# Attention, experts and a gated layer in one launch: the branch for extra tokens moves behind the first expert, and factors and weights are made during the experts

## The chip, the core and the metric

One core of one Trainium2 chip runs the whole program in one launch. The metric is the device time of an execution in microseconds (us). Engines: TensorE (PE, with PEld for its weight loads), VectorE (DVE), ScalarE (ACT), GpSimd (POOL) and SyncE (SP), which here issues nearly all DMAs.

## What is computed

```python
# 1: attention with random features: 4 batches, 8 heads, 576 tokens, 64 wide
h = x @ omega.T - sum(x * x) / 2;  phi = exp(h - max(h)) / sqrt(128)
x = (q_p @ (k_p.T @ v)) / (q_p @ sum(k_p) + 1e-6)       # 2304 tokens x 512
# 2: 8 experts, each token goes to one
e = argmax(normed(x) @ normed(emb).T / tau);  gate = softmax at e
x = gate * (relu(x @ w1[e]) @ w2[e])                     # w1 512 x 1024
# 3: gated layer; its weights are float64
g = x @ w_gate                                           # 512 x 1536
out = (g / (1 + exp(-g)) * (x @ w_val)) @ w_out          # 1536 x 512
```

All matrix products of the three layers that matter here are made from high and low parts: each factor is split into a hi part of a shorter mantissa and a lo part, and three matmuls (hi hi, hi lo, lo hi) stand for one.

## The kernel before

**Layer 1** runs in an order written out by hand and is not touched. Everything behind it is ordered, engine by engine, by the framework's scheduler, which simulates the program with a model of costs and can move an instruction far ahead of its place in the code; within an engine the order is then fixed. Buffers are tiles of pools: a load into a tile waits for the last reader of the tile before it.

**Layer 2.** The tokens are 4 blocks `bt` of S = 576 (one batch each). A block has a dominant expert, and all its tokens go through that expert with a gate of 0 where they belong to another (`expert`, L871). An expert is 8 units: 4 of `mm1` (L828) and 4 of `mm2` (L851), each with 48 matmuls of 288 columns and with one pair of loaded weights (`fetch`, `pair_tile`; hi by ACT at L90, lo by DVE at L91). ACT makes relu's hi and DVE its lo (L844, L845). Behind each mm2 DVE multiplies by the gate: into y_f at once (L869), or, where y_f is added to (`add`), into t, which POOL adds (L866, L867).

Tokens of a block that belong to other experts are the extra tokens: they are computed in a branch, `tc.If(totals[0] > 0)` (L940), with loops over blocks and experts inside. With the data of the runs shown the branch isn't taken. All engines meet at it. It stands ahead of the last block's expert, whose y_f is zeroed before it.

**Layer 3** uses a scheme of seven products for a 2 x 2 split of features and tokens. `split_y(bt)` (L883) makes seven factors of a block of x from y_f by four differences, each factor as hi (ACT) and lo; the lo and the differences of blocks 0 and 1 are POOL's, those of 2 and 3 DVE's but for two. `convert` (L729) turns a 128 x 512 piece of doubles, loaded as pairs of 32-bit words into a buffer of the experts' weights (tag raw), into float32 by eight DVE operations. `seven` (L776) makes the seven factors of the first weights of one f (12 chunks f of 128 hidden features): sums on POOL, hi on ACT, lo on POOL. Then `tokens` (L994): for each f, blocks in two pairs, seven products of six matmuls of 288 columns (L1041); DVE adds results from PSUM (L1006, L1012), ACT copies and takes silu, POOL makes one addition of two (L1013), and the hidden values go to DRAM (`hds`). The output phase reads them back (`hidden`, L1069), splits them (hi ACT, lo POOL) and multiplies them by the third weights (L1080), 8 + 8 + 2 tiles of 128 tokens, 512 columns; the third weights are converted during the first 8.

Of the kernel before, what the change touches and what calls it, by code (L numbers as in the profile page):

```python
# [27 lines left out]
def attention_moe_ffn_kernel(  # L28
# [688 lines left out]
    h_all = hpool.tile([128, F // 128 * 2 * S], F32R, name="h_all")  # L717
    LAST = B - 1

    def factor(bt, q, a):  # L720
        at = ((bt * 7 + q) * 2 + a) * S
        for v in (arena, h_all, late.get("x")):
            if at < v.shape[1]:
                return v[:, at:at + S].rearrange("p (c n) -> p c n", c=2)
            at -= v.shape[1]

    wf = {}

    def convert(dst, f, m):  # L729
# [2 lines left out]
        nc.sync.dma_start(
            out=raw, in_=w64[f, m].bitcast(I32).rearrange("p (n w) -> p n w", w=2)
        )
        t, a = (late["cpool"].tile([128, DM], I32, tag=k, name="cv_" + k) for k in "ta")
        low, high = raw[:, :, 0], raw[:, :, 1]
        nc.vector.tensor_scalar(  # L737
            out=t, in0=high, scalar1=0x7FFFFFFF, scalar2=None, op0=ALU.bitwise_and
        )
        nc.vector.scalar_tensor_tensor(  # L740
            out=high.bitcast(F32), in0=t.bitcast(F32), scalar=F64_LEAST,
            in1=high.bitcast(F32), op0=ALU.is_ge, op1=ALU.mult,
        )
# [434 lines left out]
```

## Time and profile before

| what | value |
| --- | --- |
| median of 3 runs | 842.24 us (840.14 to 843.22) |
| the profiled execution | 841.22 us |
| its span | 839.5 us |
| PE busy | 784.8 us, 93% |
| DVE busy | 555.1 us, 66% |
| POOL busy | 348.7 us, 42% |
| ACT busy | 340.0 us, 41% |
| mean granted clock of PE | 0.974 |

The span runs from the first to the last instruction of the execution on the core; the rest of its time lies around it. Busy shares are means over stages with different limits, so the stages have to be read apart. A granted clock of 1.00 is TensorE's upper level (2.4 GHz), 0.50 the lower one (1.2 GHz). In rows of a timeline the bracket gives the idle time before the instruction and what ended it; DVEq, ACTq and PEq stand for the sequencers of the engines, at a branch above all. Matmuls overlap, so the duration of a group is not its pitch.

### The profile page before, as it was taken

The page shows a single profiled execution, that of the slowest core. Times are in us where ns is not written, and L with a number is a line of the kernel's source. Part 1 is how long each engine was busy: PE and PEld are TensorE (multiplying, and loading weights), DVE is VectorE, ACT ScalarE, POOL GpSimd, SP SyncE. Part 2 cuts the span into 40 slices and gives each one's busy share as a digit, 9 for nine tenths or more (in the row PEclk, how much of TensorE's full clock was granted, in tenths as well). Part 3 has the DMA queues.
Part 4 walks back from the last instruction along what each step waited for, and adds up shares of the span by engine and source line. Part 5 has one row for each costly group of instructions (what it writes and reads, how often), then busy time and mean ns, then how long its engine had stood idle before and what let it go on. Part 6 is the DMA issues. An engine that isn't in the chain of part 4 may idle for free.

```text
span 839.5 us, 16157 instructions
## 1 busy us (share of the span) xinstructions
PE 784.8 (93%) x6364; PEld 729.2 (87%) x6365; DVE 555.1 (66%) x947; ACT 340.0 (41%) x823; POOL 348.7 (42%) x347
## 2 busy tenths in 40 slices
PE   9999899899999987986988889999999999789998
PEld 8878777899999987986988889999999987568886
DVE  6788998563424328868999977877893589960000
ACT  5887687331313222524333334444434522232123
POOL 4855253200000018765755635555555534234441
PEclk9999999999999998997999999999999999999999
DMA  8645540423223212510423333232231435335224
GB/s 282 201 143 176 186 157 22 115 78 90 86 92 90 79 32 75 135 52 0 128 83 102 109 111 95 103 107 93 109 116 73 143 122 159 140 113 183 86 68 150
DMA packets 35644, 94.13 MB, mean 112 GB/s; under 512 B 4432, under 2 KB 8544, under 8 KB 35560
## 3 DMA queue, kind: packets, MB, share of 16 engines
q1 hardware_dynamic: 35400, 92.99, 34.6%
q8 instruction: 52, 0.85, 0.4%
q14 instruction: 32, 0.26, 0.1%
q10 hardware_dynamic: 160, 0.02, 0.0%
HBM read 74.05 MB, written 18.95 MB: 111 GB/s over the span
## 4 chain that ended last, share of the span: by engine, by line
PE 32%; DVE 19%; issue 5%; POOL 3%; DMA 2%; ACT 1%; DVEq 0%; ACTq 0%; POOLq 0%; SPq 0%
PE a L1041 11%; PE o_ps L1080 10%; PE b L1041 5%; PE c L1041 3%; DVE cv_t L744 2%; DVE cv_a L748 2%; DVE cv_t L754 2%; DVE raw L740 2%; DVE cv_t L758 2%; PE two L857 2%; DVE cv_t L737 1%; POOL wl L91 1%; DVE raw L751 1%; DVE h_all L91 1%; DMA hds<-cc 1%
## 5 line engine op out<-in xcount | busy, mean ns | idle before, releaser
L1080 PE MATMUL o_ps<-xp 128*128 128x512 f32 x648 | 152.1, 397 | 8.2 <-ACT xp L90 7.9
L1080 PEld LDWEIGHTS o_ps<-xp 128*128 128x128 f32 x648 | 123.5, 191 | 36.6 <-ACT xp L90 10.0
L1041 PE MATMUL a<-xp,wh 128*128 128x288 f32 x432 | 92.4, 306 | 18.3 <-DVE c L1006 6.5
L91 POOL TENSOR_TENSOR xp<-h,xp 128x1024 fp32r<-128x1024 f32 (+1 forms) x36 | 67.1, 1866 | 101.4 <-ACT xp L90 101.4
L838 PE MATMUL two<-xp,wp 128*128 128x288 f32 x576 | 85.6, 309 | 9.5 <-ACT wp L90 4.7
L838 PEld LDWEIGHTS two<-xp,wp 128*128 128x128 f32 x576 | 82.8, 200 | 10.3 <-ACT wp L90 4.9
L91 POOL TENSOR_TENSOR xp<-y_f,xp 128x576 fp32r<-128x576 f32 x14 | 23.6, 1708 | 162.8 <-ACT xp L90 162.8
L491 ACT ACTIVATE ph<-two,bias 128x128 f32<-128x128 f32 x288 | 78.1, 387 | 29.5 <-DVE bias L482 23.2
L1041 PEld LDWEIGHTS a<-xp,wh 128*128 128x128 f32 x432 | 70.9, 194 | 21.5 <-DVE c L1006 8.0
L1009 ACT ACTIVATE cc<-cc 128x288 f32<-128x288 f32 x96 | 42.4, 445 | 106.6 <-DVE cc L1006 88.5
L1013 POOL TENSOR_TENSOR cc<-c,cc 128x288 f32<-128x288 f32 x48 | 45.7, 963 | 93.6 <-ACT cc L1009 91.0
L91 POOL TENSOR_TENSOR wl<-w,wh 128x512 fp32r<-128x512 f32 (+1 forms) x48 | 63.3, 1329 | 34.0 <-ACT wh L90 29.2
L90 ACT CAST wp<-raw 128x1024 fp32r<-128x1024 f32 x32 | 33.6, 1050 | 81.3 <-PE two L857 37.5
L1041 PE MATMUL a<-xp,wl 128*128 128x288 f32 x216 | 64.7, 303 | 0.2 <-POOL wl L91 0.2
L90 ACT CAST xp<-h 128x1024 fp32r<-128x1024 f32 (+1 forms) x36 | 30.1, 837 | 64.5 <-PE o_ps L1080 48.2
L857 PE MATMUL third<-h_all,wp 128*128 128x288 f32 x384 | 52.5, 296 | 0.0
L857 PE MATMUL two<-h_all,wp 128*128 128x288 f32 x384 | 51.8, 296 | 0.0
L857 PEld LDWEIGHTS third<-h_all,wp 128*128 128x128 f32 x384 | 51.6, 189 | 0.0
L857 PEld LDWEIGHTS two<-h_all,wp 128*128 128x128 f32 x384 | 51.4, 189 | 0.0
L474 DVE TENSOR_REDUCE mx<-two 128x8 f32<-128x1024 f32 x36 | 43.9, 1220 | 8.2 <-PE two L464 8.0
L91 DVE TENSOR_TENSOR wp<-raw,wp 128x1024 fp32r<-128x1024 f32 x30 | 40.3, 1344 | 12.5 <-ACT wp L90 11.8
L786 POOL TENSOR_TENSOR w<-w 128x256 f32<-128x256 f32 x48 | 44.6, 929 | 2.5
(199 smaller groups left out, 1738.9 us busy)
## 6 DMA issues: line engine op xcount, KB each, us to landing
raw<-in_w_dram SPq DMA_DIRECT2D x68, 512.0 KB, 3.6
hds<-cc SPq DMA_DIRECT2D x48, 288.0 KB, 2.1
h<-hds SPq DMA_DIRECT2D x24, 512.0 KB, 3.5
q<-in_qx_dram SPq DMA_DIRECT2D x18, 512.0 KB, 3.8
k<-in_kx_dram SPq DMA_DIRECT2D x14, 512.0 KB, 4.3
v<-in_vx_dram SPq DMA_DIRECT2D x18, 276.0 KB, 4.4
out_dram<-o SPq DMA_DIRECT2D x18, 256.0 KB, 3.4
h<-hds SPq DMA_DIRECT2D x12, 128.0 KB, 2.1
```

Of the source, the lines that this page charges most:

```text
L90: nc.scalar.copy(hi, src)
L91: lo_eng.tensor_tensor(out=lo, in0=src, in1=hi.bitcast(F32), op=ALU.subtract)
L474: nc.vector.tensor_reduce(out=mx.rearrange("p (c a) -> p a c", a=2), in_=p.rearrange("p a (h m) -> p a h m", m=M), axis=AX.X, op=ALU.max,)
L491: nc.scalar.activation(out=ph[:, h, :], in_=p[:, h % 2, h // 2 * M:(h // 2 + 1) * M], func=AF.Exp, bias=bias[:, h:h + 1],)
L740: nc.vector.scalar_tensor_tensor(out=high.bitcast(F32), in0=t.bitcast(F32), scalar=F64_LEAST, in1=high.bitcast(F32), op0=ALU.is_ge, op1=AL ...
L786: nc.gpsimd.tensor_tensor(out=out, in0=x, in1=y, op=op)
L838: nc.tensor.matmul(ps[:, j], w[:, a, c, f * 128:(f + 1) * 128], xv[:, c, b, j * HB:(j + 1) * HB], start=(c == 0 and n == 0), stop=(c == NC ...
L857: nc.tensor.matmul(ps[:, j], w[:, a, f, :], h[:, b, j * HB:(j + 1) * HB], start=(f == 0 and n == 0), stop=(f == len(hs) - 1 and n == 2),)
L1009: nc.scalar.activation(out=x, in_=x, func=AF.Silu)
L1013: nc.gpsimd.tensor_tensor(out=cc[:, 1], in0=c22, in1=cc[:, 1], op=ALU.mult)
L1041: nc.tensor.matmul(bank_of[k], wf[f][a][:, (wq * 2 + c) * 128:(wq * 2 + c + 1) * 128], factor(bt, xq, x)[:, c], start=(k not in begun), st ...
L1080: nc.tensor.matmul(p, h[:, x, i * 128:(i + 1) * 128], wos[f][:, a], start=(f == 0 and k == 0), stop=(f == NF - 1 and k == 2),)
```

## The change

Five things. The branch moves from ahead of the last expert to behind the matmuls of the first one (a hook ahead of its last gating), and y_f of blocks 1 to 3 is zeroed early, so that experts 1 to 3 all take the way with t and POOL's addition. The factors of x of block 0, 1, 2 are made during expert 1, 2, 3, in place of inputs that are no longer needed (`over_x`, `over_h`, `over_y`); those of block 3 behind expert 3; all lo and differences are DVE's. `convert` takes two doubles at once: one ACT operation (absolute value) and six DVE operations of 1024 columns; it has a buffer of its own. The first weights' lo moves from POOL to DVE. The first weights of f = 0 and 1 are converted during the experts, f + 2 during f, and the third weights in pairs ahead of their use.

```diff
-        n_pair[0] += 1
-        own = n_pair[0] % 3 == 0 or n_pair[0] == B * (NU + NC)
-        pool = late["cpool"] if own else wpool
+        n = n_pair[0] = n_pair[0] + 1
+        pool = late["cpool"] if n == 3 or (n > 3 and n % 3 == 2) else wpool
...
-    def convert(dst, f, m):
-        raw = wpool.tile([128, DM, 2], I32, tag="raw", name="raw64")
...
+    def convert(key, *doubles):
+        raw = late["w"].tile([128, 2, DM, 2], I32, tag="raw64", name="raw64")
+        for j, (f, m) in enumerate(doubles):
+            nc.sync.dma_start(
+                out=raw[:, j], in_=w64[f, m].bitcast(I32).rearrange("p (n w) -> p n w", w=2)
+            )
+        low, high = raw[:, :, :, 0].bitcast(U32), raw[:, :, :, 1]
+        t = late["t"].tile([128, 2, DM], I32, tag="raw", name="cv_t")
+        w = w32[key] = late["w"].tile([128, 2, DM], F32, tag="w32", name="w32", bufs=2)
+        nc.scalar.activation(out=t.bitcast(F32), in_=high.bitcast(F32), func=AF.Abs)
         nc.vector.tensor_scalar(
-            out=t, in0=high, scalar1=0x7FFFFFFF, scalar2=None, op0=ALU.bitwise_and
+            out=t.bitcast(F32), in0=t.bitcast(F32), scalar1=F64_ZERO, scalar2=None, op0=ALU.max
+        )
+        nc.vector.tensor_scalar(
+            out=t, in0=t, scalar1=0x07FFFFFF, scalar2=3,
+            op0=ALU.bitwise_and, op1=ALU.logical_shift_left,
         )
         nc.vector.scalar_tensor_tensor(
...
+            out=w.bitcast(I32), in0=high, scalar=-0x40000000, in1=t,
+            op0=ALU.bitwise_and, op1=ALU.bitwise_or,
         )
         nc.vector.tensor_scalar(
...
+            out=high, in0=w.bitcast(I32), scalar1=-0x800000, scalar2=None, op0=ALU.bitwise_and
         )
         nc.vector.scalar_tensor_tensor(
...
+            out=t.bitcast(F32), in0=low, scalar=2.0 ** -52, in1=high.bitcast(F32),
+            op0=ALU.mult, op1=ALU.mult,
+        )
+        nc.vector.tensor_tensor(out=w, in0=w, in1=t.bitcast(F32), op=ALU.add)
...
+    def weights_ahead(f):
+        if f < NF:
+            convert(f, (f, 0), (f, 1))
...
-            hi_lo(*(p[:, q * half:q * half + n] for p in parts), src, nc.gpsimd)
+            hi_lo(*(p[:, q * half:q * half + n] for p in parts), src)
...
             for d in range(NC):
-                mm2(x, hs, d, add)
+                ps = mm2(x, hs)
                 hooks.get(NU + d, lambda: None)()
+                gated(x, ps, d, add or (x.bt == 0 and d == NC - 1))
...
-            eng = nc.vector if bt >= LAST - 1 else nc.gpsimd
...
+        def extras():
+            xs[1].fetch()
+            routed.close()
...
+            with tc.If(totals[0] > 0):
...
+            nc.gpsimd.memset(y_f[0][:, NC - 1], 0.0)
+            for bt in range(1, B):
+                nc.gpsimd.memset(y_f[bt], 0.0)
...
+        todo = {
+            (0, 0): routing_end, (0, NU + NC - 1): extras,
+            (1, NU - 1): split0,
+            (2, 0): lambda: weights_ahead(0), (2, NU - 1): split1,
+            (3, 0): lambda: weights_ahead(1), (3, NU - 1): split2, (3, NU + 2): lambda: seven(0),
+        }
...
+        next(ends[2], None)
+        split(3, [over_h(r) for r in range(2, 16)])
+        next(ends[3], None)
...
                 if bt == 0 and f + 1 < NF:
-                    wf[f + 1] = seven(weights_of(f + 1, sp), parts_of(f + 1))
+                    seven(f + 1)
+                elif bt == 0:
+                    out_weights(0)
+                else:
+                    weights_ahead(f + 2)
+                    if f + 2 >= NF:
+                        out_ahead(2 * (f + 2 - NF))
...
                         if f not in wos:
-                            out_weights(f, op)
+                            out_weights(f)
+                        if f % 2 == 0:
+                            out_ahead(f + 4)
```

Which instructions stand where is settled by the scheduler. VectorE's order just ahead of the branch, before (the last lines of expert 2; L91 the lo of weights, L869 gating, L922 and L940 the branch):

```order
L869 TENSOR_TENSOR y_f<-two,gate 128x576
L91 TENSOR_TENSOR wp<-raw,wp 128x1024
L869 TENSOR_TENSOR y_f<-two,gate 128x576
L91 TENSOR_TENSOR wp<-raw,wp 128x1024
L869 TENSOR_TENSOR y_f<-third,gate 128x576
L922 TENSOR_LOAD tot_i
L940 COMPARE_AND_BRANCH
```

And after (the last lines of expert 0; L93 the lo of weights, L876 gating, L753 to L771 the six operations of a conversion, w_6254 its result, L939 and L926 the branch):

```order
L876 TENSOR_TENSOR y_f<-two,gate 128x576
L93 TENSOR_TENSOR wp<-raw,wp 128x1024
L753 TENSOR_SCALAR cv_t<-cv_t 128x1024
L756 TENSOR_SCALAR cv_t<-cv_t 128x1024
L760 SCALAR_TENSOR_TENSOR w_6254<-raw_6250,cv_t 128x1024
L876 TENSOR_TENSOR y_f<-two,gate 128x576
L93 TENSOR_TENSOR wp<-raw,wp 128x1024
L764 TENSOR_SCALAR raw_6250<-w_6254 128x1024
L767 SCALAR_TENSOR_TENSOR cv_t<-raw_6250 128x1024
L771 TENSOR_TENSOR w_6254<-w_6254,cv_t 128x1024
L939 TENSOR_LOAD tot_i
L926 COMPARE_AND_BRANCH
```

The last gating of the expert has left the place ahead of the branch, and a conversion stands there; that of f = 1, w_6254, is its last operation.

SyncE's queue ahead of the branch, before (L374 the experts' weights, L922 and L940 the branch):

```order
L374 DMA raw<-in_w_dram 128x1024
L363 TENSOR_LOAD dom_i
L374 ISA
L374 DMA raw<-in_w_dram 128x1024
L374 ISA
L374 DMA raw<-in_w_dram 128x1024
L922 TENSOR_LOAD tot_i
L940 COMPARE_AND_BRANCH
```

And after (L375 the experts' weights, raw_5749, raw_6250 and raw_6990 the doubles of f = 0, 1 and 2, L939 and L926 the branch):

```order
L327 DMA gts<-gt_t 72x128
L746 DMA raw_5749<-in_w_dram 128x1024 x2
L364 TENSOR_LOAD dom_i
L375 ISA
L375 DMA raw<-in_w_dram 128x1024
L375 ISA
L375 DMA raw<-in_w_dram 128x1024
L746 DMA raw_6250<-in_w_dram 128x1024 x2
L746 DMA raw_6990<-in_w_dram 128x1024 x2
L939 TENSOR_LOAD tot_i
L926 COMPARE_AND_BRANCH
```

Three pairs of doubles, 512 KB each double, now stand ahead of the branch.

VectorE's order at the end of the last expert and the products' start, before (L866 the gating into t, L894 and L91 differences and lo of the factors of x, L1006 the products' first addition):

```order
L894 TENSOR_TENSOR y_f<-y_f 128x2x288 x2
L91 TENSOR_TENSOR h_all<-y_f,h_all 128x576 x2
L866 TENSOR_TENSOR t<-third,gate 128x576
L894 TENSOR_TENSOR y_f<-y_f 128x2x288
L91 TENSOR_TENSOR x_late<-y_f,x_late 128x576
L894 TENSOR_TENSOR y_f<-y_f 128x2x288
L91 TENSOR_TENSOR h_all<-y_f,h_all 128x576 x2
L894 TENSOR_TENSOR y_f<-y_f 128x2x288 x2
L91 TENSOR_TENSOR x_late<-y_f,x_late 128x576
L737 TENSOR_SCALAR cv_t<-raw_6834 128x512
L1006 TENSOR_TENSOR cc<-c,s_6714 128x288
```

And after (L873 the gating into t, wl the lo of the first weights of f = 0, L902 and L93 of h_all differences and lo, w_6994 the conversion of f = 2, L1019 the products' first addition):

```order
L93 TENSOR_TENSOR h_all<-y_f,h_all 128x576
L873 TENSOR_TENSOR t<-third,gate 128x576
L93 TENSOR_TENSOR wl<-w_5753,wh 128x512
L760 SCALAR_TENSOR_TENSOR w_6994<-raw_6990,cv_t 128x1024
L902 TENSOR_TENSOR y_f<-y_f 128x2x288
L764 TENSOR_SCALAR raw_6990<-w_6994 128x1024
L93 TENSOR_TENSOR h_all<-y_f,h_all 128x576 x2
L1019 TENSOR_TENSOR cc<-c,s_6737 128x288
L767 SCALAR_TENSOR_TENSOR cv_t<-raw_6990 128x1024
L1019 TENSOR_TENSOR cc<-c,s_6752 128x288
L93 TENSOR_TENSOR h_all<-y_f,h_all 128x576
```

The first weights' lo and a conversion now lie among the factors of the last block, and the products' first additions begin between them; the gating into t stands behind a lo of the weights and one of a factor.

## Rows read from the trace of the kernel before

**Rows 1.** the page: its first line; two groups, with count, busy, mean ns

```profile
span 839.5 us, 16157 instructions
...
L1013 POOL TENSOR_TENSOR cc<-c,cc 128x288 f32<-128x288 f32 x48 | 45.7, 963 | 93.6 <-ACT cc L1009 91.0
...
L786 POOL TENSOR_TENSOR w<-w 128x256 f32<-128x256 f32 x48 | 44.6, 929 | 2.5
```

**Rows 2.** windows: stretch, busy PE, PEld, DVE, ACT, POOL, then PEclk, DMA share, GB/s

```profile
200.00:250.00 50.00, 50.00 (x378) 50.00 (x377) 18.90 (x20) 13.16 (x16) 0.00 (x0) 1.00 0.32 88
...
400.00:500.00 100.00, 90.05 (x641) 86.64 (x639) 95.22 (x153) 34.46 (x89) 56.80 (x51) 0.98 0.33 105
```

**Rows 3.** TensorE's timeline at stages and pauses: start, us, operation, idle before

```profile
206.67 6.56 PE L838 MATMUL two<-xp,wp 128*128 128x288 f32 x48
...
313.09 9.01 PE L838 MATMUL two<-xp,wp 128*128 128x288 f32 x48 [3.93 <-DVEq L940]
...
333.17 1.33 PE L838 MATMUL two<-xp,wp 128*128 128x288 f32 x4 [4.67 <-ACT wp L90]
...
380.75 0.85 PE L1041 MATMUL a<-xp,wh 128*128 128x288 f32 x2 [5.17 <-DVE t L866]
...
393.34 0.70 PE L1041 MATMUL a<-xp,wh 128*128 128x288 f32 x2 [3.32 <-ACT s L1028]
...
477.81 0.54 PE L1041 MATMUL a<-xp,wh 128*128 128x288 f32 x2 [1.99 <-DVE c L1006]
...
675.41 2.90 PE L1080 MATMUL o_ps<-xp 128*128 128x512 f32 x12
...
748.41 3.92 PE L1080 MATMUL o_ps<-xp 128*128 128x512 f32 x16 [0.35 <-ACT xp L90]
```

**Rows 4.** ScalarE's timeline at the end: the last copy of the output

```profile
835.83 0.58 ACT L1087 COPY o<-o_ps 128x512 f32<-128x512 f32 x1 [4.39 <-PE o_ps L1080]
```

**Rows 5.** windows behind two pauses, and one of the output phase

```profile
313.00:318.00 5.00, 4.91 (x20) 4.94 (x21) 1.22 (x1) 1.99 (x4) 5.00 (x5) 0.50 0.61 213
...
480.00:485.00 5.00, 5.00 (x32) 5.00 (x31) 4.97 (x10) 1.15 (x4) 2.01 (x2) 0.77 0.12 16
...
700.00:720.00 20.00, 16.27 (x67) 12.71 (x66) 19.49 (x22) 5.34 (x7) 8.93 (x4) 0.94 0.45 153
```

**Rows 6.** VectorE's timeline, and one POOL operation beside it at 681.98

```profile
201.56 1.23 DVE L91 TENSOR_TENSOR wp<-raw,wp 128x1024 fp32r<-128x1024 f32 x1 [0.33 <-ACT wp L90]
...
677.87 0.69 DVE L91 TENSOR_TENSOR xp<-wo,xp 128x512 fp32r<-128x512 f32 x1
...
678.47 0.42 DVE L744 TENSOR_SCALAR cv_t<-raw 128x512 int32<-128x512 int32 x1
...
678.92 0.69 DVE L748 SCALAR_TENSOR_TENSOR cv_a<-raw,cv_t 128x512 int32<-128x512 int32 x1
...
681.98 2.54 POOL L91 TENSOR_TENSOR xp<-h,xp 128x1024 fp32r<-128x1024 f32 x1 [5.76 <-ACT xp L90]
...
682.29 2.50 DVE L737 TENSOR_SCALAR cv_t<-raw 128x512 int32<-128x512 int32 x1
```

**Rows 7.** VectorE and ScalarE around the branch (L940 is the branch)

```profile
309.20 0.76 DVE L869 TENSOR_TENSOR y_f<-third,gate 128x576 f32<-128x576 f32 x1 [4.09 <-PE third L857]
...
311.45 3.54 ACT L90 CAST xp<-y_f 128x576 fp32r<-128x576 f32 x6 [7.60 <-PEq L940]
```

**Rows 8.** SyncE's queue behind the branch: the doubles, then the experts' weights

```profile
313.01 1.11 SPq L732 DMA_DIRECT2D raw<-in_w_dram  x2
...
328.55 6.20 SPq L374 DMA_DIRECT2D raw<-in_w_dram  x2
```

**Rows 9.** VectorE's groups by form: count, busy, mean ns

```profile
L1006 DVE TENSOR_TENSOR cc<-b,u 128x288 f32<-128x288 f32 x48 | 21.6, 453 | 5.3 <-PE b L1041 5.3
...
L894 DVE TENSOR_TENSOR y_f<-y_f 128x576 f32<-128x576 f32 x8 | 11.4, 1425 | 0.1
...
L91 DVE TENSOR_TENSOR h_all<-y_f,h_all 128x576 fp32r<-128x576 f32 x6 | 9.5, 1617 | 0.7 <-ACT h_all L90 0.7
```

More of the change, by code (lines that the diff above doesn't have):

```diff
@@ L717, in attention_moe_ffn_kernel @@
     h_all = hpool.tile([128, F // 128 * 2 * S], F32R, name="h_all")
+    ypool = ctx.enter_context(tc.tile_pool(name="ypool", bufs=B, reuse_waits="tile"))
+    y_f = [ypool.tile([128, NC * S], F32, tag="y", name="y_f") for _ in range(B)]
+    y_f = [y.rearrange("p (c n) -> p c n", c=NC) for y in y_f]
     LAST = B - 1
-    def factor(bt, q, a):
[L721 to L725, printed above, removed]
@@ L727, in attention_moe_ffn_kernel @@
-    wf = {}
-    def convert(dst, f, m):
-        raw = wpool.tile([128, DM, 2], I32, tag="raw", name="raw64")
[L732 to L736, printed above, removed]
-        nc.vector.tensor_scalar(
-            out=t, in0=high, scalar1=0x7FFFFFFF, scalar2=None, op0=ALU.bitwise_and
[L739 to L742, printed above, removed]
+    parts_at = [[] for _ in range(B)]
@@ L950, in attention_moe_ffn_kernel @@
-        w0 = weights_of(0, tp)
-        def first_seven():
-            wf[0] = seven(w0, parts_of(0))
-        def whole(bt):
-            for _ in split_y(bt):
-                pass
-        end = {bt: split_y(bt) for bt in (LAST - 1, LAST)}
-        hooks = {0: lambda: whole(0), NU - 1: lambda: whole(1), NU: lambda: next(end[LAST - 1])}
-        hooks[NU + 2] = first_seven
-        expert(last, True, hooks)
-        routed.close()
-        late["x"] = routed.enter_context(
-            tc.tile_pool(name="x_late", bufs=1, side="right", reuse_waits="tile")
-        ).tile([128, B * 14 * S - B * XB - F // 128 * 2 * S], F32R, name="x_late")
@@ L966, in attention_moe_ffn_kernel, with ahead, split @@
-        next(end[LAST - 1])
-        next(end[LAST])
-        next(end[LAST], None)
-        next(end[LAST - 1], None)
-        next(end[LAST], None)
+            nc.gpsimd.memset(y_f[0][:, NC - 1], 0.0)
+            for bt in range(1, B):
+                nc.gpsimd.memset(y_f[bt], 0.0)
+        def ahead(bt):
+            xs[bt - 1].fetch()
+            xs[bt] = Expert(bt)
+            xs[bt].fetch()
+        def split(bt, runs):
+            parts_at[bt] += runs
+            ends.append(split_y(bt))
+            next(ends[-1])
@@ new lines, in split0, with split1, split2 @@
+        def split0():
+            split(0, [over_x(0, r) for r in range(8)] + [over_x(1, r) for r in range(6)])
+            next(ends[0], None)
+        def split1():
+            own = [over_x(1, 6), over_x(1, 7)] + runs_of(over_y())
+            split(1, own + [over_x(2, r) for r in range(8)])
+            next(ends[1], None)
+        def split2():
+            own = runs_of(over_y()) + [over_x(3, r) for r in range(8)]
+            split(2, own + [over_h(0), over_h(1)])
+        todo = {
[4 more added lines that the diff above has]
+        }
@@ L972, in attention_moe_ffn_kernel @@
+        for bt in range(B):
+            hooks = {u: go for (b, u), go in todo.items() if b == bt}
+            if bt < LAST:
+                hooks[NU + NC - 2] = lambda: ahead(bt + 1)
+            expert(xs[bt], bt > 0, hooks)
+        next(ends[2], None)
+        split(3, [over_h(r) for r in range(2, 16)])
+        next(ends[3], None)
+        late["odd"] = [over_y() for _ in "hl"]
+    late["t"] = wpool
     banked.close()
```

148 lines of the change are left out of this document (59 added, 89 removed).

## Prediction

> **What bounds the kernel now.** I read the span first: 839.5 us [rows 1]. The run of that profile took 841.22 us, so 1.7 us lie around the span, and the median of the runs shown, 842.24, is 1.0 above it. The sum below is made against 841.2; the 1.0 is added at the end.
>
> Then the windows of the experts and of the gated layer [rows 2]. In 200 to 250 us TensorE (PE) is busy all 50.00 us at full clock, with VectorE (DVE) at 18.90: a stretch bound by PE alone. In 400 to 500 PE is busy 90.05 of 100 while DVE is at 95.22 and GpSimd (POOL) at 56.80: there DVE is the bound.
>
> Then TensorE's timeline [rows 3], which cuts the span into stages. Call the four experts E0 to E3. E0 ends at 206.67, E2 at 313.09 - 3.93 = 309.16: 768 matmuls in 102.49 us, 51.2 us for an expert's 384, 0.1333 each. E3 ends at 380.75 - 5.17 = 375.58, so E3 with the branch ahead of it takes 66.4 us, 15.2 over its matmuls. The products end where the first matmul on o_ps starts, 675.41: 299.8 us, against 2016 x 0.1333 = 268.8 for their matmuls (12 f x 4 blocks x 7 products x 6, of the same 288 columns), so 31.0 are lost. The output phase has 648 matmuls; from 748.41, where 384 are left, to the last copy at 835.83 [rows 4] they run with nothing between them: 87.4 us, 0.2275 each, 147.4 for all. It takes 160.4 to that copy: 13.0 lost, all before 748.41, and there DVE is busy 19.49 of 20 us [rows 5]. Together 15.2 + 31.0 + 13.0 = 59 us that are not matmuls at full rate.
>
> **The change, part by part.**
>
> *Up to E0's end: no change.* The instructions stand in the same order until E0's second half. There DVE gets two conversions of a pair of doubles (12 operations) ahead of the branch. E1 and the stretch before show what room there is: DVE 18.90 of 50 [rows 2]. The second conversion waits for 1 MB of doubles that is asked for once the first has read its buffer. I lay the operations behind the rows of DVE there, the last lo of an expert's weights at 201.56 (1.23 us, [rows 6]) among them: the second conversion ends near 206.3, just ahead of PE's 206.67. If the doubles came 2 us later, the branch would be 2 us later, no more.
>
> *The branch, 15.2 now.* Its parts are [rows 3, 5, 7, 8]: all engines meet at it. DVE's gating of E2's last tile (309.20, 0.76 us) ends 0.8 us after PE; PE starts again 3.1 us after that, at 313.09; ScalarE (ACT) passes at 311.45, 2.3 us after PE's end. Then the first 48 matmuls take 9.01 us instead of 6.4, with a granted clock of 0.50 in 313 to 318 (1.2 of 2.4 GHz): 2.5 lost. Then SyncE (SP) issues the doubles at 313.01, and their buffers are those of the experts' weights, so the next weights go out at 328.55 and PE waits 4.67 us at 333.17. The rest of the 15.2 (about 4 us) is the slow clock after that wait and small pauses.
> Now the last gating stands behind the branch and the doubles have a buffer of their own, so the 0.8 and the 4.67 go. PE can start again at the later of its own end + 2.3 and DVE's last + 3.1: 206.3 + 3.1 = 209.4, a pause of 2.7 (bounds 2.3, ACT's value, and 3.93 as now). The clock: a pause of 3.93 cost 2.5 us; those of 1.99 and a few tenths at 477.81 [rows 3] left a clock of 0.77 in the 5 us behind them [rows 5], 1.2 us. I take 1.5 between them. What is late next: SP passes the branch only when the third pair of doubles, asked for just ahead of it (about 205), has landed, near 210.5; weights of the unit after next then land near 217, PE needs them at 209.4 + 12.8 + its slow start, 223 or so. That is 6 us of cover; without it the price would be a wait such as the 4.67. Branch: 4.2.
>
> *E1 to E3: 153.6.* Per expert DVE gets, beside its 18.9, a set of factors of x (7 lo and 4 differences of 576 columns, taken at the 0.76 of the gating [rows 7], 8.4 us) and a conversion: 33 of 51.2. POOL's additions now run in three experts, 4 each. PE stays the bound.
>
> *The conversion.* Two doubles took 16 DVE operations of 512 columns; now 6 of 1024 and one on ACT. Of 1024 columns the trace has only the lo of a weight (1.23), a two-input operation like the three of the new code; with 0.69 for 512 [rows 6] that is 0.54 for each 512 columns and 0.15 besides. A one-input operation of 512 takes 0.42; it isn't there with 1024: bounds 0.42 and 0.84, I take 0.15 + 2 x 0.27 = 0.69. Conversion: 3 x 0.69 + 3 x 1.23 = 5.8 us, where it was 9.4 alone.
>
> *The products.* For one f DVE has this conversion 5.8, the lo of the weights that leave POOL (512 columns 0.69 [rows 6], three and a half: 2.5), and 16 operations that read PSUM, 0.45 each [rows 9], 7.2: 15.5. PE needs 168 x 0.1333 = 22.4. POOL keeps four additions and four multiplications of 0.93 and 0.96 [rows 1]: 7.6 at their means. Beside a POOL operation of 2.54 us at 681.98 a DVE operation of 0.42 took 2.50 [rows 6]; if all of POOL's time were taken from DVE, 15.5 + 7.6 = 23.1. But those that read PSUM keep 0.45 in the mean, so only the other 8.3 can be hit, and DVE stays under 22.4. PE becomes the bound: 268.8.
> At the products' start PE still waits, as now (5.17 [rows 3]), for the gating of the last tile on DVE. It stands behind two lo of 0.7 there, which can begin before PE's end; I take 3.0 and a clock loss of 1.2. The factors of the fourth block, the rest of a conversion and the first weights' lo all fall into f = 0, some 15 us of DVE against 11.2 of PE's first pair of blocks: 4.0. What in before cost 3.32 at 393.34 is within it. Bounds of this: 2 (the wait alone) to 20 (rival D). Start 8.2, products 277.0.
>
> *Output.* It converts six pairs. Four of them now lie ahead of the products' end, in f = 10 and 11, where no first weights are converted any more: 4 x 5.8, 32 additions at 0.45 and some 4 us of lo are 41.6 us of DVE in 44.8 of PE. Two are left, 11.6 us beside the 43 us of PE in which their weights come up. Of the 13.0 lost I leave 0.5: 147.9, with up to 5 more if POOL's lo of the hidden values (2.54 each, [rows 6]) stretches them.
>
> **Sum.** 206.7 + 4.2 + 153.6 + 277.0 + 147.9 = 789.4; from the last copy to the span's end 839.5 - 835.8 = 3.7: 793.1; around the span 1.7: 794.8. Against 841.2: 11.0 at the branch, 22.8 in the products, 12.5 in the output. With the 1.0 of the median: 796.
>
> **Rivals.**
>
> *B, DVE stays the bound of the products.* PE would be busy 90.05 of 100 as now [rows 2], 268.8 / 0.9005 = 298.5, 29.7 more, less the 4.0 already counted: 821. For it: conversions, lo and additions share one queue, in which an addition waits behind an operation of 1.23. Against: 15.5 of 22.4, and POOL loses the lo of the weights.
>
> *C, the branch costs at its new place what it did at the old*, 15.2: 807. It decides itself at SP's first weights behind the branch: issued later than about 219, they are late for PE. For it: 3 MB of doubles and the weights share the queues just ahead.
>
> *D, the factors come too late.* All lo and differences are on DVE; beside POOL a lo took 1.62 and a difference 1.43 in the mean [rows 9]. The fourth block's set would take 7 x 1.62 + 4 x 1.43 = 17 instead of 8.4, and PE would stand for 9 more with a loss of clock of 2.5: 807.
> The Trainium skill (GPSIMD Engine Reference, section 8, Key points) says that GpSimd shares its SBUF interfaces with VectorE, with contention where a DVE instruction has two SBUF inputs or a two-port mode; this speaks against bringing the lo to DVE. The trace agrees (0.42 became 2.50), and by that rule D is what happens wherever POOL is busy in f = 0; its four additions there are short, so I leave D small.
>
> *E, slower.* In every f DVE falls behind far enough that PE pauses as at the branch, 3.93 and 2.5 of clock: 6.4 x 12 - 4 = 73 more, 869. It decides at DVE's need for one f: above 22.4 + 3.9 = 26.3 us, for which the conversion would have to take 16.6 instead of 5.8, if for instance its pairs of interleaved words cost thrice at 1024 columns. The time would be as before where each f loses (46.4 + 4.0) / 12 = 4.2, a pause of 2.7 with 1.5 of clock: DVE at 25.1.
>
> **How the numbers follow.** Forecast 0.66, with a range of its own of 786 (pause 2.3, start 2, output 0) to 806 (start and output at 5 more each); B 0.08, C 0.10, D 0.11, E 0.05, of which 0.02 stop within 0.5% of before, about what a measurement of this kernel can tell from no change. The range takes in C and D, which leaves out B, E and a tenth of the forecast: 786 to 815. Faster 0.66 + 0.08 + 0.10 + 0.11 = 0.95, same 0.02, slower 0.03.
>
> **What the profile of after would show.** The span's first 206 us unchanged; behind E0 a pause of 2.3 to 4 us and a clock near 0.5 for a few us at most; no pause between E1 and E3; E3's end near 364; one pause of 2 to 4 us at the products' start, then PE 20.00 in windows of 20; DVE near 70% there, with 1024-column operations at 0.69 and 1.23; products' end near 641, output near 148. The prediction is wrong if E3 ends after 372, if one f takes more than 23 us, or if the conversion takes more than 8.5.

## Result: faster, and ten microseconds behind the sum

The changed kernel takes 802.91 us (median of 4 runs, 798.64 to 807.0) against 841.19 of the kernel before: a ratio of 0.9545, interval 0.9484 to 0.9607. 796 was forecast, with a range of 786 to 815. The profiled execution took 804.78 us against a sum of 794.8, so 10.0 us are to be found in it.

Its page, first line and the two groups of POOL:

```profile
span 803.0 us, 15964 instructions
...
L1026 POOL TENSOR_TENSOR cc<-c,cc 128x288 f32<-128x288 f32 x48 | 51.9, 1089 | 161.2 <-ACT cc L1022 160.9
...
L796 POOL TENSOR_TENSOR w<-w 128x256 f32<-128x256 f32 x48 | 38.2, 795 | 18.8 <-DVE wl L93 12.8
```

TensorE's timeline of after, at the same stages as [rows 3]:

```profile
165.88 2.61 PE L250 MATMUL one<-xp,en_st 128*128 128x384 f32 x7 [6.68 <-DVE xp L598]
...
215.62 8.61 PE L842 MATMUL two<-xp,wp 128*128 128x288 f32 x48 [4.55 <-DVEq L926]
...
373.87 0.82 PE L1054 MATMUL a<-xp,wh 128*128 128x288 f32 x2 [2.45 <-DVE t L873]
...
428.89 0.54 PE L1054 MATMUL a<-xp,wh 128*128 128x288 f32 x2 [1.15 <-ACT u L1043]
...
645.20 1.81 PE L1054 MATMUL a<-h_all,over_y 128*128 128x288 f32 x6 [3.91 <-ACT u L1043]
...
651.49 10.86 PE L1094 MATMUL o_ps<-xp 128*128 128x512 f32 x47
```

ScalarE's last copy ([rows 4]):

```profile
799.37 0.59 ACT L1101 COPY o<-o_ps 128x512 f32<-128x512 f32 x1 [4.39 <-PE o_ps L1094]
```

A stage ends where the next row's start less its pause lies: expert 0 at 215.62 - 4.55 = 211.07, expert 3 at 371.42.

| stage, us | before | forecast | after | after - forecast |
| --- | --- | --- | --- | --- |
| to expert 0's end | 206.7 | 206.7 | 211.1 | +4.4 |
| to expert 3's end | 168.9 | 157.8 | 160.4 | +2.6 |
| products | 299.8 | 277.0 | 280.1 | +3.1 |
| output, to the last copy | 160.4 | 147.9 | 147.9 | 0 |
| to the span's end | 3.7 | 3.7 | 3.6 | 0 |

Windows of after (columns as in [rows 2]): inside the products TensorE is busy nearly all the time with VectorE at 11 to 15 of 20 from 420 to 620, where it was at 95 of 100 [rows 2].

```profile
460.00:480.00 20.00, 20.00 (x153) 20.00 (x152) 12.59 (x23) 9.78 (x23) 6.61 (x8) 1.00 0.26 96
480.00:500.00 20.00, 20.00 (x152) 20.00 (x152) 11.30 (x24) 9.58 (x23) 5.32 (x7) 1.00 0.28 105
...
640.00:650.00 10.00, 6.09 (x30) 5.86 (x29) 9.66 (x15) 3.86 (x8) 4.50 (x4) 0.66 0.71 265
```

The last of them is the loss at the products' end: a pause, and TensorE at 0.50 behind it. [rows 2] show the worse part of the products before. From 520 to 600 us TensorE ran without a pause there too; one of those windows of the kernel before:

```profile
540.00:560.00 20.00, 20.00 (x153) 20.00 (x152) 15.53 (x29) 9.37 (x24) 11.58 (x12) 1.00 0.29 94
```

So the products were not bound by VectorE throughout, and what the change gained lies in the other stretches. VectorE's groups of after by form give the conversion:

```profile
L760 DVE SCALAR_TENSOR_TENSOR w<-raw,cv_t 128x1024 int32<-128x1024 int32 x18 | 27.2, 1512 | 0.3
L767 DVE SCALAR_TENSOR_TENSOR cv_t<-raw 128x1024 f32<-128x1024 uint32 x18 | 24.7, 1373 | 0.1
L771 DVE TENSOR_TENSOR w<-w,cv_t 128x1024 f32<-128x1024 f32 x18 | 23.3, 1293 | 0.2
...
L764 DVE TENSOR_SCALAR raw<-w 128x1024 int32<-128x1024 int32 x18 | 16.5, 916 | 0.1
...
L756 DVE TENSOR_SCALAR cv_t<-cv_t 128x1024 int32<-128x1024 int32 x18 | 13.3, 737 | 0.4
L753 DVE TENSOR_SCALAR cv_t<-cv_t 128x1024 f32<-128x1024 f32 x18 | 12.5, 692 | 18.0 <-ACT cv_t L752 17.9
```

The six means sum to 6.5 us; 5.8 was taken. Where POOL is idle, single operations take 0.69 and 1.23, as forecast.

Where the 4.4 us ahead of expert 0's end come from is seen at the end of attention, in VectorE's and POOL's timelines of after:

```profile
155.89 6.59 DVE L171 TENSOR_SCALAR ny<-ss 128x9 int32<-128x9 int32 x1 [0.74 <-ACT x L587]
```

```profile
155.99 0.58 POOL L942 MEMSET y_f<- 128x576 f32 x1
156.51 5.95 POOL L944 MEMSET y_f<- 128x2304 f32 x3
```

An operation on 9 columns lasts 6.59 us, until POOL's row of memsets is over (162.46). The scheduler had put the zeroing of y_f there. In the kernel before the same operation took 2.15 us, with one memset of 2.02:

```profile
155.90 2.15 DVE L169 TENSOR_SCALAR ny<-ss 128x9 int32<-128x9 int32 x1 [0.73 <-ACT x L586]
```

```profile
156.00 2.02 POOL L939 MEMSET y_f<- 128x2304 f32 x1
```

### The profile page after: what moved, and what is told of

Same layout as the page of the kernel before. It is cut to its first block, busy times and chain, and to the rows that moved or that the text cites. A ratio compares the mean times of both kernels' runs of the same rounds, so it can differ in the third digit from the quotient of the medians.

```text
span 803.0 us, 15964 instructions
## 1 busy us (share of the span) xinstructions
PE 769.9 (96%) x6364; PEld 720.8 (90%) x6365; DVE 485.0 (60%) x841; ACT 363.2 (45%) x841; POOL 262.7 (33%) x285
## 4 chain that ended last, share of the span: by engine, by line
PE 63%; DVE 3%; POOL 2%; issue 2%; DMA 2%; ACT 1%; SPq 0%; POOLq 0%; ACTq 0%; DVEq 0%
PE o_ps L1094 16%; PE a L1054 16%; PE b L1054 8%; PE two L842 7%; PE two L861 5%; PE third L861 4%; PE c L1054 4%; PE third L842 2%; POOL w L796 1%; DMA hds<-cc 1%; DMA raw<-in_w_dram 1%; POOL xp L93 1%; DVE cv_t L767 1%; DMA h<-hds 0%; DVE wl L93 0%
## 5 line engine op out<-in xcount | busy, mean ns | idle before, releaser
L1094 PE MATMUL o_ps<-xp 128*128 128x512 f32 x648 | 147.5, 389 | 0.3 <-POOL xp L93 0.3
L1026 POOL TENSOR_TENSOR cc<-c,cc 128x288 f32<-128x288 f32 x48 | 51.9, 1089 | 161.2 <-ACT cc L1022 160.9
L93 POOL TENSOR_TENSOR xp<-h,xp 128x1024 fp32r<-128x1024 f32 (+1 forms) x36 | 70.1, 1954 | 86.3 <-ACT xp L92 84.4
L842 PE MATMUL two<-xp,wp 128*128 128x288 f32 x576 | 82.2, 302 | 4.5 <-DVEq L926 4.5
L874 POOL TENSOR_TENSOR y_f<-y_f,t 128x576 f32<-128x576 f32 x13 | 19.9, 1529 | 183.8 <-DVE t L873 183.8
L1054 PE MATMUL a<-xp,over_y 128*128 128x288 f32 x360 | 58.1, 295 | 0.0
L1054 PE MATMUL a<-xp,wh 128*128 128x288 f32 x240 | 50.7, 301 | 3.6 <-DVE t L873 2.5
L93 DVE TENSOR_TENSOR wp<-raw,wp 128x1024 fp32r<-128x1024 f32 x30 | 46.6, 1555 | 10.0 <-ACT wp L92 9.7
L1054 PEld LDWEIGHTS a<-xp,over_y 128*128 128x128 f32 x360 | 51.4, 188 | 0.0
L796 POOL TENSOR_TENSOR w<-w 128x256 f32<-128x256 f32 x48 | 38.2, 795 | 18.8 <-DVE wl L93 12.8
L1054 PEld LDWEIGHTS a<-xp,wh 128*128 128x128 f32 x240 | 39.4, 192 | 4.0 <-ACT wh L92 2.7
```

The source lines that it names most:

```text
L93: lo_eng.tensor_tensor(out=lo, in0=src, in1=hi.bitcast(F32), op=ALU.subtract)
L796: nc.gpsimd.tensor_tensor(out=out, in0=x, in1=y, op=op)
L842: nc.tensor.matmul(ps[:, j], w[:, a, c, f * 128:(f + 1) * 128], xv[:, c, b, j * HB:(j + 1) * HB], start=(c == 0 and n == 0), stop=(c == NC ...
L874: nc.gpsimd.tensor_tensor(out=yv, in0=yv, in1=t, op=ALU.add)
L1026: nc.gpsimd.tensor_tensor(out=cc[:, 1], in0=c22, in1=cc[:, 1], op=ALU.mult)
L1054: nc.tensor.matmul(bank_of[k], wf[f][a][:, (wq * 2 + c) * 128:(wq * 2 + c + 1) * 128], factor(bt, xq, x)[:, c], start=(k not in begun), st ...
```

## Experiments

Stage lengths of all kernels, from their profiles as above (us):

| kernel | to E0's end | to E3's end | products | output | median of its runs |
| --- | --- | --- | --- | --- | --- |
| a_again | 211.4 | 160.4 | 280.7 | 147.7 | 805.6 |
| a_memset_late | 206.1 | 162.8 | 280.1 | 147.6 | 802.0 |
| b_memset_late | 204.5 | 168.6 | 300.1 | 161.3 | 840.3 |
| a_no_branch | 211.2 | 153.8 | 279.9 | 147.2 | 798.3 |
| b_no_branch | 206.8 | 153.7 | 301.8 | 161.7 | 828.9 |
| c_conv1_late | 204.5 | 161.6 | 280.9 | 147.5 | 797.9 |
| c_end | 204.5 | 160.0 | 274.9 | 147.2 | 792.2 |
| a_lo_pool | 212.0 | 162.4 | 292.5 | 147.1 | 818.8 |
| a_conv16 | 214.2 | 158.9 | 300.4 | 148.3 | 827.4 |
| d_quiet | 206.1 | 159.4 | 275.2 | 147.2 | 793.1 |
| e_two | 204.0 | 157.7 | 275.1 | 147.2 | 794.9 |

### a_again

No edit.

> The changed kernel, unaltered, for a second profile and times on the same chip as the others. The first four runs spread from 798.6 to 807.0 us. If the stages are fixed by the program, this profile has the same ends as the first: expert 0 at 211.1, restart behind the branch 215.6, expert 3 at 371.4, products 651.5, span 803 within 1 us. If the spread of 8 us comes from one stage (the hand-ordered attention with its DMAs is the candidate), that stage alone differs, by up to 6 us, and the rest agrees within 0.5.

805.56 us (804.07 to 809.44); every stage within 0.6 us of the first profile. Where the spread of 8 us in the first four runs comes from was not found here; e_two shows a part of it.

### a_memset_late

```diff
-                nc.gpsimd.memset(y_f[bt], 0.0)
+                nc.vector.tensor_copy(y_f[bt][0:1, 0, 0:1], tot[:, 0:1]); nc.gpsimd.memset(y_f[bt], 0.0)
```

> The changed kernel with one edit: the zeroing of y_f of blocks 1 to 3 (three POOL memsets of 2.0 us) waits for the routing's total, by a one-element copy of it on VectorE. Theory M: the tiny VectorE operation L171 (128 x 9) took 6.59 us because it stood still until POOL's four memsets were over (155.9 to 162.5). Then it now lasts until the one short memset of 0.6 us is over, under 1 us; PE's pause of 6.68 at 165.9 shrinks to 2 or less; expert 0 ends at 205 to 207 instead of 211.1, and the time falls by 4 to 6 us. Rival: L171 waits for something else (ScalarE's result, a slow start of its form), it stays above 6 and the time is the same. A price is possible in both: the memsets now lie beside a lo of weights at about 183, which could be held up to 6 us and PE by up to 3.

802.01 us, ratio to before 0.9509 (0.9476 to 0.9541); 805.56 for the changed kernel on the same chip. VectorE and POOL of this run:

```profile
157.77 0.71 DVE L171 TENSOR_SCALAR ny<-ss 128x9 int32<-128x9 int32 x1 [0.73 <-ACT x L587]
```

```profile
157.88 0.58 POOL L942 MEMSET y_f<- 128x576 f32 x1
179.81 5.97 POOL L944 MEMSET y_f<- 128x2304 f32 x3 [21.36 <-DVE y_f L944]
```

6.59 became 0.71, which again ends with the memset that was left (158.46). PE's pause went from 6.68 to 1.01 and expert 0 ends at 206.1, although attention itself ran 1.9 us later in this execution. Theory M holds. No lo of a weight was held up by the moved memsets: the one at 182.15, with two inputs, took its usual 1.23 beside them, so it isn't every VectorE operation that stands. From expert 0's end to expert 3's it took 2.4 us more, which no expectation had. Expert 0 ended 5.0 us earlier, but VectorE jumped at the branch only 4.0 earlier (207.1 for 211.1) and then stood 5.6 us instead of 4.4; see d_quiet.

### b_memset_late

The same edit in the kernel before.

> The kernel before with one edit: its one zeroing of 2.0 us waits for the routing's total, as in the run with the late memset. Theory M: there too the tiny operation of the norms (L169, 2.15 us) stood until POOL's memset was over (158.02); it now takes under 0.3 or until the end of POOL's lo just before, and expert 0 ends 1.5 to 2.2 us earlier than 206.7; the time falls by about 2. Rival: 2.15 was another delay; nothing changes there.

840.33 us, ratio 0.9984 (0.9965 to 1.0003). The operation in this run:

```profile
156.31 0.20 DVE L169 TENSOR_SCALAR ny<-ss 128x9 int32<-128x9 int32 x1 [0.74 <-ACT x L586]
```

2.15 became 0.20 and expert 0 ends at 204.5 instead of 206.7, as theory M had it. The trace shows the mechanism. The medians differ by 2.3 us, but the interval of the ratio just includes no change.

### a_no_branch and b_no_branch

Both leave out the extra tokens' experts and the load of their total.

> The changed kernel without the branch (the extra tokens' experts are left out; with this data the branch isn't taken). Theory: the branch costs what stands between expert 0's end and expert 3's end over the 153.6 of matmuls: pause 4.55 and 2.2 of slow clock, 6.8; that stretch becomes 153.6 to 154.5 and the time falls by 6 to 7 us. Rival: the branch only collects waits that come anyway (weights late, conversions ahead of gatings), then the stretch falls by 3 at most and pauses show at other places of expert 1.

> The kernel before without its branch ahead of the last expert (extra tokens' experts left out; not taken with this data). The prediction put the whole 15.2 us that expert 3 takes over its matmuls on the branch and what it brings with it. If that holds, the stretch from expert 2's end (309.2) to expert 3's end falls from 66.4 to 51.2 to 53 and the time by 13 to 15. Rival: pause and clock alone belong to the branch, 3.9 + 2.5; the wait of 4.67 for weights (their buffers are lent to the doubles) and what follows from it stay: the stretch falls by 6 to 8, to about 59.

798.33 us (0.9487, 0.9464 to 0.9511), 7.2 under the changed kernel on the same chip; 828.85 us (0.9838, 0.9818 to 0.9857), 13.8 under before. From expert 0's end to expert 3's the matmuls alone are left, 153.8 and 153.7: the branch and what hung on it cost 15.2 us at its old place, as the prediction read it, the wait of 4.67 behind the doubles' loan of buffers included, and 6.6 at the new one, where 4.2 was taken. Neither rival came.

### c_conv1_late

On top of a_memset_late (lines that only hand the new argument on are left out):

```diff
+        if after is not None: nc.gpsimd.tensor_copy(raw[0:1, :, 0, 0].bitcast(F32), after)
...
-            (3, 0): lambda: weights_ahead(1), (3, NU - 1): split2, (3, NU + 2): lambda: seven(0),
+            (3, 0): lambda: weights_ahead(1, y_f[0][0:1, 3, 0:2]), (3, NU - 1): split2, (3, NU + 2): lambda: seven(0),
```

> The changed kernel with the zeroing behind the routing (as in the run with the late memset) and with the doubles of f = 1 made to wait for the first block's factors, so that neither their conversion nor the third pair's load stands ahead of the branch. Theory F: what follows a taken branch has to be fetched, and the fetch is slow beside the load of 1 MB: VectorE stood 4.4 us between its jump (211.1) and its next operation (215.5), 5.6 in the run with the late memset, 3.1 in the kernel before with empty queues; PE waits for VectorE's. Then VectorE now jumps a good 1 us ahead of PE's end and stands 2.5 to 3.2 us, PE's pause is 1.9 to 2.6, the slow clock costs 1.2 to 2, and from expert 0's end to expert 3's end it takes 157 to 158 us instead of 160.4 (162.6 with the late memset); the time is 4 to 5 us under that of the late memset. Rival: the pause is the branch's own and hangs neither on the loads nor on the conversion; it stays 4.5 or more.

797.87 us (0.9464, 0.9435 to 0.9494). The median is 4.1 under a_memset_late's 802.01, as expected, but the stretch behind expert 0 is 161.6, only 1.2 shorter than there and not the 157 to 158 of theory F. The sequencers at the branch in the changed kernel (first and last start, us):

```profile
L926 PEldq EVENT_SEMAPHORE  x2: 51/51/51, 212.6 to 212.8; - x2
L926 DVEq EVENT_SEMAPHORE  x2: 21/21/21, 215.5 to 215.6; - x2
...
L926 PEldq COMPARE_BRANCH  x1: 3372/3372/3372, 209.1 to 209.1; - x1
L926 DVEq COMPARE_BRANCH  x1: 72/72/72, 211.1 to 211.1; - x1
```

and in this run, with TensorE's timeline behind it:

```profile
L926 DVEq EVENT_SEMAPHORE  x2: 21/21/21, 203.0 to 203.1; - x2
L926 PEldq EVENT_SEMAPHORE  x2: 51/51/51, 206.7 to 206.9; - x2
...
L926 DVEq COMPARE_BRANCH  x1: 72/72/72, 199.8 to 199.8; - x1
```

```profile
207.12 1.43 PE L842 MATMUL two<-xp,wp 128*128 128x288 f32 x9 [2.62 <-PEq L926]
211.73 7.18 PE L842 MATMUL two<-xp,wp 128*128 128x288 f32 x39 [3.18 <-issue]
```

VectorE does what theory F says: it stands 3.2 us between jump and next operation instead of 4.4, and is through well before TensorE. But TensorE then pauses 2.62 for its own branch and, after nine matmuls, 3.18 with nothing to wait for that this view shows. Together that is 5.8, the rival's "4.5 or more". Taking VectorE out of the way shows TensorE's own price.

### d_quiet

As c_end (below), with the gate's load held back:

```diff
+        later = lambda x, t: x.extra or x.bt != 1 or nc.gpsimd.tensor_copy(t[0:1, 63:65], h_all[0:1, 0:2].bitcast(F32))
...
-            t = gpool.tile([128, S], F32, tag="gate" + "x" * x.extra, name="gate")
+            t = gpool.tile([128, S], F32, tag="gate" + "x" * x.extra, name="gate"); later(x, t)
```

> As c_end, and the load of the second block's gate (288 KB in small packets) waits for that block's first hidden values, so that it no longer falls into the time in which TensorE fetches what follows the branch. Theory F': taking VectorE's conversion from ahead of the branch bought nothing because TensorE then stands by itself, 2.2 to 2.6 us at its own jump and 1.7 to 3.2 more after nine matmuls with nothing to wait for, while weights and gate land: the branch's price is fetched instructions behind loads. Without the gate's load the second pause falls under 0.7 and expert 0's end to expert 3's end takes 157.5 to 159 instead of 160.0 and 161.6. Rival: the second pause is a fixed part of a jump and stays at 1.7 to 3.2, the stretch at 160 to 162.

793.06 us (0.9404, 0.9369 to 0.944); the stretch is 159.4.

```profile
208.47 1.43 PE L842 MATMUL two<-xp,wp 128*128 128x288 f32 x9 [2.37 <-PEq L926]
211.74 6.56 PE L842 MATMUL two<-xp,wp 128*128 128x288 f32 x39 [1.84 <-issue]
```

The second pause stays at 1.84 (1.68 in c_end), so the gate's load isn't its cause; the stretch of 159.4 lies between theory F' and its rival.

The traces show where the second pause ends. Among their DMA records are packets of instructions. Those of queue q8, 16,384 bytes each, go with TensorE's work: one comes every 16 to 19 us while matmuls run without a pause (203.65 and 221.10 in a_no_branch). At the branch two of them count (us; "on" is TensorE's first step behind the branch, PEldq's EVENT_SEMAPHORE):

| kernel | first packet landed | on | second packet, start to landing | matmuls start | second pause ends |
| --- | --- | --- | --- | --- | --- |
| before | 309.56 | 311.0 | 311.96 to 312.99 | 313.09 | none |
| after | 211.07 | 212.6 | 214.49 to 215.46 | 215.62 | none |
| a_memset_late | 206.09 | 207.6 | 210.72 to 211.69 | 212.90 | none |
| c_conv1_late | 205.21 | 206.7 | 209.22 to 210.45 | 207.12 | 211.73 |
| c_end | 204.73 | 206.2 | 207.49 to 209.10 | 206.64 | 210.50 |
| d_quiet | 206.55 | 208.1 | 209.32 to 210.28 | 208.47 | 211.74 |

TensorE goes on 1.4 to 1.6 us behind the first packet, and the second pause ends 1.3 to 1.5 behind the second. Where VectorE holds TensorE up longer, the second packet has landed by the time the matmuls start (0.1 behind it in a_conv16), and no second pause shows. By these times the pause is no fixed part of a jump: TensorE waits for the next packet of instructions, and theory F' is right in that. The loads bear on when that packet starts: 0.7 to 1.2 us behind "on" with the DMA engines all but idle (before, b_memset_late, a_conv16), 1.7 to 3.1 while the doubles landed (after, a_again, a_memset_late, e_two, a_lo_pool), 1.2 to 2.5 beside other loads (the three of the table with a second pause). This is read from times that coincide in all these profiles; no run holds the packet alone back.

### c_end

On top of c_conv1_late:

```diff
-            hi_lo(h[:, 0], h[:, 1], raw, nc.gpsimd)
+            hi_lo(h[:, 0], h[:, 1], raw, nc.vector if t0 == 0 and f < 3 else nc.gpsimd)
```

> As the run before, and the lo of the first three pieces of hidden values on VectorE instead of POOL. Theory: at the products' end PE loses some 6 us (3.9 of pause at 645.2 and a clock of 0.50 behind it) because POOL's lo of the hidden values, 6.3 us for two at 634.8, stretches VectorE's operations beside it (3.08 where 1.23 is usual, 2.53 where 0.69), and the additions queue behind them. Then the pause at the end falls under 2 us and the products, from expert 3's end on, from 280 to 274 to 277. Rival: VectorE has too much work in the last f (four conversions of the output's weights), and three more operations of 1.23 make the pause as long or longer: 280 or more.

792.24 us, ratio 0.9412 (0.9395 to 0.943): the lowest median, with d_quiet's ratio of 0.9404 within the interval. VectorE and POOL at the products' end in the changed kernel:

```profile
635.72 3.08 DVE L767 SCALAR_TENSOR_TENSOR cv_t<-raw 128x1024 f32<-128x1024 uint32 x1
638.72 0.45 DVE L1019 TENSOR_TENSOR cc<-b,u 128x288 f32<-128x288 f32 x1
639.09 2.53 DVE L93 TENSOR_TENSOR xp<-w,xp 128x512 fp32r<-128x512 f32 x1
```

```profile
634.76 6.31 POOL L93 TENSOR_TENSOR xp<-h,xp 128x1024 fp32r<-128x1024 f32 x2 [2.34 <-ACT xp L92]
```

and VectorE in c_end:

```profile
628.50 1.22 DVE L767 SCALAR_TENSOR_TENSOR cv_t<-raw 128x1024 f32<-128x1024 uint32 x1
629.63 0.46 DVE L1019 TENSOR_TENSOR cc<-b,u 128x288 f32<-128x288 f32 x1
630.00 1.22 DVE L93 TENSOR_TENSOR xp<-h,xp 128x1024 fp32r<-128x1024 f32 x1
```

The operation beside POOL is back at 1.22, three more of VectorE at 1.22 to 1.46 cost it less than waiting beside POOL's did, the pause of 3.9 is gone (0.23 is left at 637.69) and the products take 274.9 instead of 280.9: 6.0, as the theory had it. The Trainium skill (GPSIMD Engine Reference, section 8, Key points) has GpSimd share its SBUF interfaces with VectorE; the rows agree, 1.22 against 3.08.

### e_two

Late zeroing and VectorE's lo of the hidden values only.

> The changed kernel with two edits only: the late zeroing, and the lo of the first three pieces of hidden values on VectorE; the conversion of f = 1 stands ahead of the branch again. If the two terms add up as measured apart (3.5 for the zeroing by the medians, 5.6 to 6 at the products' end), it lies 9 us under the changed kernel, at 793 to 796. If holding back that conversion was worth what the medians say (4 us between the runs with and without), it lies 3 to 4 above c_end's 792.2, at 795 to 797; if it was worth nothing, as the stretches behind the branch say (160.0 and 161.6 against 160.4 of the changed kernel), it is within 1.5 of it.

794.92 us (789.45 to 795.8), ratio 0.9442 (0.9422 to 0.9462), which overlaps c_end's. The terms add up: 793 to 796 was expected. What c_conv1_late's edit is worth can't be told from the times: 794.92 is 2.7 over c_end, between the 1.5 and the 3 to 4 expected, and the profiled execution here is the fastest, 789.45, for a reason of its own. TensorE's timeline of it:

```profile
261.73 6.40 PE L842 MATMUL two<-xp,wp 128*128 128x288 f32 x48
267.97 3.28 PE L842 MATMUL third<-xp,wp 128*128 128x288 f32 x24
```

48 matmuls in 6.24 us (267.97 - 261.73) where every other profile has 6.40 at the same granted clock of 1.00; over experts 1 to 3 that is 3.7 us, and without it the stretch would be 161.4, by 1.4 longer than c_end's. Why this execution was faster there is not known; its products ran at the usual pace.

### a_lo_pool and a_conv16

Each undoes one part of the change: the first weights' lo on POOL, and sixteen operations of 512 for a pair of doubles, without the one on ScalarE.

```diff
-            hi_lo(*(p[:, q * half:q * half + n] for p in parts), src)
+            hi_lo(*(p[:, q * half:q * half + n] for p in parts), src, nc.gpsimd)
```

> The changed kernel with one part undone: the lo of the first weights on POOL again. Prediction's theory: TensorE bounds the products with room to spare (VectorE 12.9 of 20 us), so 2.5 us less on VectorE and 5 us more on POOL for each f change little: products 280 to 286, the windows of 20 us from 440 to 620 still 20.00. Rival: the lo's move is what took the bound from VectorE; with POOL at 5 us more its operations stretch VectorE's to 19 of 20, pauses come back in every f, and the products take 290 to 300 as in the kernel before.

> The changed kernel with one part undone: a pair of doubles is converted by sixteen VectorE operations of 512 columns, as before, instead of one of ScalarE and six of 1024; buffers and places stay. Rows of the kernel before give 9.4 us alone and 13.7 beside POOL for the sixteen, against some 7 now: VectorE's need for one f goes from about 14.5 to 18 to 21.5 of 22.4. Theory of the prediction: the conversion is the largest part of what freed VectorE; the inner f stay TensorE's (pauses under 1 us each), but the ends don't: the branch starts 2 to 4 us later and the last f pause for 8 to 12 more, products 286 to 295, time 810 to 820. Rival: the conversion's form matters little, since its place was the trouble: time within 4 us of the changed kernel.

818.84 us (0.972, 0.9695 to 0.9744) and 827.41 us (0.9821, 0.9794 to 0.9848): 16 and 24.5 us over the changed kernel's 802.91 (13 and 22 over a_again's 805.56). The products take 292.5 and 300.4, the latter as long as before the change (299.8). Windows of a_lo_pool:

```profile
480.00:500.00 20.00, 20.00 (x150) 19.66 (x148) 10.90 (x18) 8.08 (x20) 6.86 (x8) 1.00 0.33 112
500.00:520.00 20.00, 17.87 (x124) 17.73 (x123) 12.31 (x19) 9.45 (x22) 10.68 (x11) 0.91 0.24 84
```

and of a_conv16:

```profile
460.00:480.00 20.00, 18.31 (x135) 17.84 (x135) 16.30 (x34) 6.35 (x18) 5.17 (x7) 1.00 0.32 113
480.00:500.00 20.00, 19.11 (x140) 18.38 (x139) 15.44 (x30) 7.73 (x21) 5.12 (x6) 1.00 0.25 83
```

Both expectations of the prediction's theory were too mild. For a_lo_pool the rival's 290 to 300 came, but not its reason, a VectorE at 19 of 20. From 400 to 620 us VectorE is busy 11.5 of 20 in the mean in a_lo_pool and 15.9 in a_conv16, far from full, and TensorE pauses in many f all the same. The kernel before had 15.5 of 20 in a window without a pause. So the busy share doesn't tell when VectorE's queue is late.

What makes it late can be read behind the largest inner pause of each. In a_lo_pool (VectorE, VectorE, TensorE):

```profile
494.14 0.69 DVE L753 TENSOR_SCALAR cv_t<-cv_t 128x1024 f32<-128x1024 f32 x1 [3.13 <-ACT cv_t L752]
500.99 0.46 DVE L1019 TENSOR_TENSOR cc<-c,s 128x288 f32<-128x288 f32 x1 [3.73 <-DMA hds<-cc]
502.27 1.76 PE L1054 MATMUL a<-xp,over_y 128*128 128x288 f32 x6 [2.13 <-ACT u L1043]
```

and in a_conv16:

```profile
495.24 0.43 DVE L754 TENSOR_SCALAR cv_t<-raw 128x512 int32<-128x512 int32 x1 [3.04 <-DMA raw<-in_w_dram]
506.33 0.46 DVE L1019 TENSOR_TENSOR cc<-c,s 128x288 f32<-128x288 f32 x1 [2.73 <-DMA hds<-cc]
507.60 1.61 PE L1054 MATMUL b<-xp,over_y 128*128 128x288 f32 x6 [2.17 <-ACT p L1044]
```

VectorE stands idle at a conversion whose doubles haven't landed (in a_lo_pool ScalarE's part of it waits for them). The additions behind it come late, in a_conv16 also behind the conversion's longer row of operations, so the hidden values are stored late; VectorE then waits for that store, because it needs the buffer, ScalarE waits for VectorE's addition and copies late, and TensorE waits for the copy. In all of the products VectorE waits 33.3 us for the input of conversions in a_lo_pool and 26.3 in a_conv16, against 4.9 in the changed kernel. Why the doubles are late in both, and how much of the 12 and 20 us this makes, no run of its own shows.

## Why the prediction was right, and where its sum was off

**The branch before, 15.2:** right, shown by b_no_branch. **At the new place, 4.2:** 6.6 (a_no_branch). The step that VectorE's last + 3.1 releases TensorE had the right form and the wrong size: VectorE's conversion ended at 211.66, 0.6 behind TensorE, and it came back 4.0 later, 4.4 after its jump (3.1 in the kernel before); the clock took 2.2 where 1.5 was taken. The other bound, TensorE's own end + 2.3, was too low: alone, TensorE pauses 2.2 to 2.6 and then 1.7 to 3.2 more. That 4 us could be had without the conversion ahead was my own next step; c_conv1_late's stretch is only 1.2 shorter. SyncE didn't wait for the third pair to land, as the prediction has it: it jumped at 211.8, while the pair was landing, and its next step came at 216.4.

**Up to expert 0's end, no change:** wrong by 4.4. The instructions do stand in the same order on VectorE, but POOL's memsets, counted nowhere in the sum, lie beside them. The kernel before showed the price in its own trace: 2.15 us for 9 columns (0.20 in b_memset_late).

**The products, 277.0:** the mechanism was right in the main, and rival B is out: TensorE bounds them, with 20.00 in nearly all windows. But "DVE stays under 22.4" isn't what decides it: a_conv16 has VectorE busy 15.9 of 20, under that too, and TensorE pauses. The conversion's 5.8 was 6.5. Of the 8.2 at the start only the wait for t came (2.45 for 3.0, with some slow clock), nothing of the 4.0 for late factors, so rival D is out as well; instead 3.9 and a slow clock came at the end. The step that failed is "41.6 us of DVE in 44.8 of PE": it left out POOL's lo of the hidden values, drawn into the last f, which the prediction had put into the output as up to 5 us. c_end shows it, 6.0. That the products came within 3.1 is partly luck, since the 4.0 that didn't come stands against these 6.0.

**The output, 147.9:** right to the tenth. **Rival C** (15.2 at the new place) and **E** didn't come; the first weights behind the branch went out at 217.45, ahead of C's 219, and none were late. The range's lower end of 786 doesn't follow from the terms it names: 796 less 0.4, 6.2 and 0.5 is 788.9. The time lies far above it, so nothing hung on that.

The gain of 36.5 in the profiled executions is thus 8.5 behind expert 0, 19.7 in the products and 12.5 in the output, less 4.4 for the zeroing. By a_conv16 and a_lo_pool undoing the conversion's form alone costs 20 us in the products and undoing the lo's move 12: each is needed, and they don't add, since together the change gained 19.7 there.

## What to carry to other kernels

Before zeroing or other fill work goes to an idle POOL, look at what VectorE does in that stretch, down to operations of 9 columns on a chain that TensorE waits for; give the fill a dependency that puts it elsewhere. In a queue in order, one operation that waits for a load holds up everything behind it that TensorE needs, and the busy share doesn't show it; look at what the engine is idle for. A branch costs TensorE several microseconds by itself even when its body isn't run (2.2 to 2.6 and 1.7 to 3.2 here), so its place should be chosen for what else waits and what else loads there.
